# A new emission order and 106 new engine choices for a fused attention and hard-swish MLP kernel

## The chip, the cores and the metric

The kernel runs on one core of a Trainium2 chip. The metric is the device time of one execution in microseconds (us). Three runs of the kernel before gave 426.27, 427.37 and 429.7 us; the median is 427.37 us.

## The reference

Attention over 8 sequences, 12 heads, 448 positions and 64 values per head, with RMS normalisation of queries and keys, and then a two-layer MLP with a hard-swish between the layers:

```
q_n = q / sqrt(mean(q*q) + 1e-6) * g_q          (k likewise)
a   = softmax(q_n @ k_n.T / 8) @ v
x   = a as [8*448, 12*64] = [3584, 768]
h   = x @ w_in                                   [3584, 2048]
out = (h * clip(h + 3, 0, 6) / 6) @ w_out        [3584, 768]
```

Inputs and output are float32 in DRAM; the kernel multiplies in bf16 and sums in float32.

## The kernel before, in words

**Units of work.** Two heads of a sequence make a pair; a sequence has 6 pairs, so pairs P0 to P47 cover the 8 sequences. For a pair, `load` (L417, on the SP queue) fetches k, q and v. `square` (L359 on ACT, L361 on POOL) and a reduction on DVE (L446, L480) give sums of squares, `roots` (L422, L425, on ACT) turns them into factors, and `scale` (L364, on POOL or DVE) writes the normalised bf16 values `qks`. They are turned by TensorE and an identity (L534) for P0 to P12, from P13 on by a transposing DMA on the SP queue (L553, tile T); k is then multiplied by the gains (`kt`, L561 on ACT, L563 on DVE). `score` (L586; L609 in the first sequence) multiplies k by q: two matmuls, one for each head, each on 64 of TensorE's 128 rows. ACT takes the exponential (L592, L614). `av` (L672, L631) multiplies by v with a column of ones, DVE divides (L688, L691), and the result goes into `xT` through TensorE (L656, L707) for the first two sequences and through a transposing DMA (L698) after that.

**The MLP.** `h_group` (L764; L745 in the first sequence) multiplies `w_in` by `xT` in steps of three 448-column matmuls. ACT and DVE apply the hard-swish (L723, L726) into `gT`. `y_group` (L786) multiplies by `w_out` in steps of four 384-column matmuls, ACT or DVE copies the sums out (L345, L347), and the SP queue stores them (L807). The weights come in four parts each, through DMAs that POOL issues (L817, L822); a part of `w_in` serves four of the 16 column blocks of h.

**The first sequence** (P0 to P5) is handled apart: its queries are cut into two halves (z = 0, 1) so that scores can start when half of q is there. 30 groups of four matmuls on zeros (`warm`, L377) stand at the start; some more on zeros (`idle`, L370) stand ahead of `av_first`.

**What sets the order.** Nothing is scheduled at run time. The kernel first makes a list of 2386 plan entries (`Plan.add`), each with its dependencies and the engines that it may run on. `Plan.emit` (L193) then walks a list written out by hand, `ORDER` (L35), and issues each entry on the engine that `WAY` (L23) picks: the first of its list when it has no number there, otherwise the one at that number. The engines take their instructions strictly in that order; semaphores make them wait for one another. The SP queue carries the loads, the transposing DMAs and the stores, also in order.

```python
    def emit(self, order):
        ...
        for i in order:
            kind, engines, fn, preds = self.ops[i]
            fn(engines[WAY.get(i, 0)])
```

The entries that matter below: 0 to 3 are the four parts of `w_in` and 4 to 7 those of `w_out`; 212, 230 and 250 square the second half of q for P0, P2 and P5, 122 the first half for P4; 126 scales the k of P4 and 154 the first half of q for P5; 509 is the exponential of the first score step of P7; 904 is the DMA that turns the result of P17, the last pair of the third sequence, into `xT`.

Of the kernel before, what the change touches and what calls it, by code (L numbers as in the profile page):

```python
# [23 lines left out]
    53: 1, 63: 2, 68: 1, 69: 1, 78: 2, 83: 1, 84: 1, 95: 1, 100: 1, 101: 2, 121: 1, 127: 1, 148: 1, 212: 1,  # L24
    214: 1, 230: 1, 232: 1, 241: 1, 250: 1, 326: 1, 346: 1, 366: 2, 386: 1, 387: 1, 496: 2, 525: 1, 544: 1,
    560: 2, 583: 1, 589: 2, 617: 1, 624: 1, 637: 1, 664: 1, 770: 1, 879: 1, 880: 1, 886: 1, 921: 1, 954: 1,
    1005: 1, 1010: 1, 1017: 1, 1024: 1, 1067: 1, 1108: 2, 1125: 1, 1151: 1, 1160: 1, 1166: 2, 1274: 1, 1286:
    1, 1317: 1, 1324: 1, 1335: 1, 1344: 1, 1350: 1, 1370: 1, 1376: 1, 1393: 1, 1402: 1, 1445: 1, 1469: 1,
    1474: 1, 1530: 1, 1553: 1, 1572: 2, 1598: 1, 1615: 1, 1630: 1, 1641: 1, 1650: 1, 1673: 1, 1708: 1, 1714:
    1, 1754: 1, 1785: 1, 1817: 1, 1822: 1, 1865: 1, 1872: 2, 1891: 1, 1898: 2, 1909: 1, 1918: 1, 1924: 1,  # L30
    1949: 1, 1956: 1, 1972: 1, 1973: 1, 1979: 1, 1987: 1, 2016: 1, 2039: 1, 2067: 1, 2072: 1, 2095: 1, 2114:
    2, 2136: 1, 2151: 1, 2159: 1, 2174: 1, 2195: 1, 2313: 1, 2333: 1, 2374: 1,
# [3 lines left out]
    9, 20, 8, 21, 22, 11, 23, 10, 24, 25, 13, 28, 26, 14, 27, 53, 17, 31, 55, 32, 16, 33, 54, 212, 12, 34,  # L36
    56, 57, 58, 35, 68, 92, 61, 213, 36, 59, 18, 70, 60, 29, 69, 62, 214, 91, 73, 71, 84, 37, 119, 64, 72,
    30, 38, 76, 83, 65, 66, 39, 145, 40, 67, 74, 215, 104, 75, 118, 102, 85, 77, 79, 103, 41, 120, 94, 81,
    80, 15, 86, 82, 95, 63, 129, 87, 225, 105, 42, 89, 96, 43, 44, 19, 88, 130, 131, 93, 108, 110, 111, 109,
    97, 112, 146, 98, 106, 132, 100, 113, 45, 99, 107, 135, 121, 114, 156, 115, 158, 148, 136, 122, 116,  # L40
    133, 157, 46, 117, 90, 134, 47, 123, 149, 159, 172, 164, 0, 48, 150, 124, 230, 174, 125, 165, 232, 49,
    78, 126, 151, 166, 216, 50, 173, 167, 233, 51, 52, 127, 152, 160, 217, 175, 154, 162, 161, 137, 138,
    163, 139, 153, 231, 188, 190, 168, 189, 169, 178, 218, 179, 176, 170, 140, 191, 177, 128, 220, 141, 200,
    221, 219, 142, 234, 201, 202, 171, 143, 340, 227, 192, 193, 144, 203, 194, 101, 195, 224, 303, 155, 196,
    222, 261, 304, 180, 223, 248, 305, 197, 226, 181, 182, 235, 250, 249, 183, 236, 228, 306, 315, 184, 271,
    185, 237, 238, 147, 272, 316, 239, 186, 198, 339, 240, 187, 247, 199, 317, 251, 204, 318, 245, 205, 360,
    341, 327, 244, 307, 308, 252, 206, 241, 309, 253, 207, 328, 242, 273, 254, 208, 329, 209, 246, 255, 256,
    330, 310, 210, 243, 347, 359, 211, 311, 274, 342, 257, 348, 260, 349, 312, 319, 320, 258, 229, 321, 343,
    313, 350, 322, 344, 314, 370, 323, 331, 324, 371, 372, 361, 1, 325, 326, 374, 373, 332, 275, 345, 259,
    351, 375, 333, 352, 334, 362, 353, 363, 354, 335, 386, 397, 364, 336, 376, 398, 355, 337, 263, 377, 276,  # L50
    365, 338, 399, 387, 356, 401, 357, 400, 264, 402, 378, 2, 379, 358, 500, 388, 346, 380, 403, 405, 489,
    501, 406, 381, 407, 265, 404, 408, 266, 389, 382, 277, 409, 490, 502, 383, 506, 390, 410, 503, 384, 267,
    411, 268, 391, 412, 507, 385, 278, 504, 508, 3, 505, 366, 512, 283, 513, 509, 392, 491, 510, 535, 284,
    511, 524, 514, 269, 515, 516, 517, 285, 554, 270, 537, 525, 518, 286, 519, 492, 279, 553, 493, 520, 538,
    521, 280, 393, 555, 522, 281, 291, 495, 536, 292, 523, 282, 494, 539, 498, 293, 543, 526, 287, 367, 544,
    540, 541, 368, 288, 542, 395, 294, 527, 566, 289, 564, 497, 545, 556, 528, 290, 546, 567, 530, 547, 394,
    299, 565, 262, 548, 529, 300, 549, 533, 550, 295, 301, 582, 532, 551, 583, 302, 570, 296, 531, 552, 572,
    571, 421, 297, 4, 573, 568, 593, 298, 569, 595, 6, 584, 413, 414, 594, 415, 618, 422, 423, 416, 596,
    574, 417, 646, 418, 575, 557, 419, 576, 577, 585, 617, 559, 601, 578, 599, 420, 602, 424, 425, 579, 426,
    558, 429, 427, 430, 600, 428, 5, 580, 607, 431, 433, 581, 647, 432, 605, 597, 560, 437, 598, 608, 438,  # L60
    496, 434, 439, 606, 586, 630, 435, 440, 603, 587, 628, 604, 436, 445, 619, 7, 441, 631, 446, 588, 629,
    648, 609, 442, 447, 636, 634, 443, 448, 610, 611, 620, 649, 444, 612, 650, 621, 453, 637, 613, 622, 635,
    614, 659, 657, 652, 449, 658, 450, 623, 454, 451, 660, 615, 455, 738, 663, 616, 452, 632, 748, 737, 750,
    633, 458, 561, 739, 638, 562, 456, 591, 639, 457, 640, 396, 641, 740, 749, 465, 625, 642, 643, 466, 664,
    369, 769, 644, 751, 499, 467, 645, 651, 534, 661, 754, 756, 662, 468, 654, 770, 459, 626, 469, 771, 665,
    590, 666, 757, 667, 760, 668, 477, 821, 669, 772, 670, 773, 741, 460, 755, 589, 743, 671, 478, 672, 461,
    796, 746, 563, 752, 462, 742, 479, 753, 655, 470, 795, 761, 780, 758, 782, 759, 774, 797, 480, 471, 783,
    822, 777, 762, 624, 763, 786, 764, 775, 481, 765, 472, 781, 766, 767, 473, 653, 823, 768, 853, 808, 474,
    784, 806, 482, 776, 824, 785, 812, 483, 854, 787, 825, 809, 484, 745, 485, 880, 627, 798, 788, 486, 789,
    790, 799, 807, 677, 801, 678, 744, 791, 804, 679, 832, 792, 834, 826, 488, 833, 680, 673, 747, 793, 674,  # L70
    835, 800, 813, 685, 675, 827, 803, 810, 879, 840, 676, 838, 844, 686, 811, 855, 681, 687, 682, 839, 779,
    688, 814, 815, 829, 683, 816, 817, 856, 656, 693, 857, 841, 818, 858, 684, 794, 694, 819, 689, 828, 695,
    836, 820, 696, 864, 837, 690, 881, 866, 691, 842, 778, 701, 843, 692, 1050, 870, 702, 845, 867, 697,
    1049, 703, 698, 830, 882, 1017, 846, 704, 859, 592, 847, 848, 865, 1051, 709, 896, 699, 892, 890, 883,
    893, 849, 700, 885, 710, 850, 861, 1052, 851, 705, 711, 1018, 862, 706, 871, 891, 831, 712, 868, 884,
    1030, 1053, 707, 1028, 888, 1019, 717, 869, 860, 887, 718, 708, 852, 1101, 872, 719, 873, 874, 1031,
    875, 720, 713, 802, 1040, 876, 1029, 714, 877, 1102, 725, 897, 715, 1020, 1034, 716, 894, 1021, 1036,
    1022, 895, 1103, 721, 722, 1035, 1076, 1025, 898, 878, 899, 723, 900, 1055, 1037, 901, 724, 726, 902,
    1104, 1054, 903, 1060, 727, 729, 1061, 728, 904, 730, 1023, 1041, 1032, 731, 1062, 1075, 733, 464, 1063,
    732, 734, 1066, 1033, 1077, 905, 735, 1088, 1038, 1058, 1086, 736, 1039, 906, 476, 909, 1078, 1057,  # L80
    1079, 1105, 910, 907, 1081, 1026, 1042, 908, 911, 1043, 1044, 1080, 1087, 913, 912, 1045, 1089, 1133,
    914, 1124, 1046, 1047, 917, 1067, 1106, 918, 915, 463, 1024, 916, 1159, 1064, 1084, 1112, 1114, 1065,
    919, 1092, 1134, 1160, 922, 1068, 1135, 1048, 920, 1113, 1069, 1070, 921, 886, 1118, 1083, 1161, 1136,
    1071, 1286, 923, 889, 924, 863, 1093, 1162, 1318, 1119, 925, 1072, 1073, 1125, 929, 1107, 926, 930,
    1115, 927, 1082, 933, 805, 1285, 931, 934, 1317, 932, 1120, 1144, 1137, 935, 1090, 1138, 937, 1150,
    1091, 936, 938, 1163, 941, 1164, 939, 475, 1094, 940, 1095, 1085, 1121, 1139, 1096, 1097, 1287, 945,
    1110, 1056, 1109, 946, 1098, 1288, 1165, 1145, 1099, 1167, 942, 1319, 1074, 1151, 1146, 1116, 1170, 943,
    947, 1117, 944, 487, 948, 1108, 1320, 1142, 1289, 1321, 1122, 1290, 949, 950, 1100, 1123, 957, 1343,
    1344, 1126, 1308, 1127, 1128, 1345, 1171, 1129, 951, 1147, 952, 1176, 1130, 1131, 953, 1296, 1168, 954,
    1172, 1148, 1141, 958, 1149, 961, 955, 959, 962, 928, 1323, 1370, 960, 1152, 1132, 963, 1153, 1309,  # L90
    1154, 1291, 1297, 1155, 965, 1156, 964, 1173, 966, 1401, 1177, 969, 967, 1157, 970, 968, 1298, 1174,
# [862 lines left out]
```

## Time and profile before

| | us |
|---|---|
| median of three runs | 427.37 |
| the profiled execution | 427.26 |
| its span, first to last instruction | 425.2 |
| PE (matmul) busy | 415.3 |
| ACT busy | 292.1 |
| DVE busy | 220.6 |
| POOL busy | 179.9 |

PE is TensorE's matmuls and PEld its weight loads; DVE is VectorE, ACT ScalarE, POOL GpSimd, SP SyncE. A matmul's recorded duration includes its way through the array, so that neighbours overlap in the records: what a step of PE costs is read from start to start, not from its duration. The granted TensorE clock was full over the whole span. The other 2.1 us of the execution lie around the span.

### The profile page before, as it was taken

The numbers are of one execution on the slowest core, as the hardware profiler recorded it, in microseconds if no ns is written. First come the engines' busy times: TensorE is split into PE (matmuls) and PEld (weight loads), VectorE is DVE, ScalarE is ACT, GpSimd is POOL, SyncE is SP. The second block draws the span as 40 slices with busy tenths as digits, with TensorE's granted clock in tenths as the row PEclk, the third lists the DMA queues.
The fourth block names the chain that finished last, engine by engine and source line by source line (L and its number), as shares of the span: only waits on it lengthen the run. The fifth ranks groups of instructions, "written<-read, shape, count | busy, mean of one in ns | idle before, by whom it ended". The sixth has DMA issues, their size and how long they took to land.

```text
span 425.2 us, 10132 instructions
## 1 busy us (share of the span) xinstructions
PE 415.3 (98%) x4050; PEld 248.5 (58%) x4050; DVE 220.6 (52%) x438; ACT 292.1 (69%) x533; POOL 179.9 (42%) x205
## 2 busy tenths in 40 slices
PE   7899999999999999999999999999999999999996
PEld 6665887554555555555555565555555555655564
DVE  5878777447965664545454555464434432233300
ACT  6899887789998886796867766587865842143211
POOL 4899777685876544446061472223410300000000
PEclk9999999999999999999999999999999999999999
DMA  7999999979969978665765348928530412101214
GB/s 252 295 270 257 225 237 179 298 196 238 246 158 215 243 197 206 158 178 146 164 184 168 69 108 184 239 64 212 124 75 11 113 49 67 49 2 47 66 40 145
DMA packets 98930, 67.76 MB, mean 159 GB/s; under 512 B 53156, under 2 KB 95428, under 8 KB 98884
## 3 DMA queue, kind: packets, MB, share of 16 engines
q1 hardware_dynamic: 93248, 60.50, 55.2%
q0 software_dynamic: 5248, 6.29, 8.9%
q8 instruction: 31, 0.51, 0.5%
q10 hardware_dynamic: 388, 0.34, 0.3%
q14 instruction: 15, 0.12, 0.1%
HBM read 50.23 MB, written 11.01 MB: 144 GB/s over the span
## 4 chain that ended last, share of the span: by engine, by line
PE 79%; DMA 8%; ACT 4%; DVE 3%; POOL 2%; issue 2%; SPq 1%; DVEq 0%; ACTq 0%; POOLq 0%
PE M L786 26%; PE M L764 24%; PE X L672 8%; PE S L586 5%; PE S L786 5%; PE M L745 4%; PE X L586 2%; DMA w_in_sb<-in_moe_w_in_dram 2%; ACT eT L614 2%; DMA gT<-in_q_dram 2%; DMA T<-qks 2%; PE X L764 1%; DMA qk<-in_k_dram 1%; POOL sq L361 1%; PE S L764 1%
## 5 line engine op out<-in xcount | busy, mean ns | idle before, releaser
L786 PE MATMUL M<-w_out_sb,gT 128*128 128x384 bf16 x752 | 137.8, 326 | 0.0
L364 POOL TENSOR_TENSOR qks<-qk,rs 112x512 bf16<-112x512 f32 (+1 forms) x90 | 91.5, 1030 | 104.2 <-ACT rs L425 57.9
L764 PE MATMUL M<-xT,w_in_sb 128*128 128x448 bf16 x618 | 134.4, 353 | 0.4 <-ACT y L345 0.2
L726 DVE SCALAR_TENSOR_TENSOR gT<-ts,M 128x448 bf16<-128x448 f32 x119 | 73.1, 617 | 90.4 <-ACT ts L723 89.4
L786 PEld LDWEIGHTS <-gT 128*128 128x128 bf16 x912 | 84.2, 98 | 57.7 <-issue 7.2
L592 ACT ACTIVATE eT<-S 112x896 bf16<-112x896 f32 x112 | 100.0, 916 | 7.7 <-PE S L586 5.0
L764 PEld LDWEIGHTS <-w_in_sb 128*128 128x128 bf16 x672 | 60.3, 98 | 57.8 <-issue 11.7
L723 ACT ACTIVATE ts<-M 128x448 f32<-128x448 f32 x119 | 64.6, 544 | 40.1 <-PE M L764 29.6
L361 POOL TENSOR_TENSOR sq<-qk 112x512 f32<-112x512 f32 (+1 forms) x60 | 60.7, 1019 | 40.0 <-DVE ssq L446 12.4
L592 ACT ACTIVATE eT<-X 112x896 bf16<-112x896 f32 x56 | 51.4, 918 | 17.6 <-PE X L586 16.8
L672 PEld LDWEIGHTS <-eT 112*128 112x128 bf16 x1344 | 53.2, 97 | 15.7 <-issue 2.2
L672 PE MATMUL X<-va,eT 112*128 112x65 bf16 x1344 | 56.8, 194 | 0.0
L446 DVE TENSOR_REDUCE ssq<-sq 112x16 f32<-112x1024 f32 x42 | 50.8, 1213 | 10.5 <-POOL sq L361 7.3
L586 PE MATMUL S<-T 64*128 64x448 bf16 x224 | 35.6, 353 | 0.0
L345 ACT COPY y<-M 128x384 f32<-128x384 f32 x28 | 13.4, 479 | 28.9 <-PE M L786 24.5
L691 DVE TENSOR_TENSOR xn<-X,rd 112x512 bf16<-112x512 f32 x42 | 28.9, 689 | 1.1
L586 PEld LDWEIGHTS <-T 64*128 64x128 bf16 x336 | 12.6, 94 | 24.4 <-issue 18.5
L745 PE MATMUL M<-xT,w_in_sb 128*128 128x224 bf16 x192 | 23.1, 259 | 0.6 <-DMA w_in_sb<-in_moe_w_in_dram 0.3
L347 DVE COPY y<-M 128x384 f32<-128x384 f32 x19 | 10.5, 554 | 25.2 <-PE M L786 21.5
L359 ACT ACTIVATE sq<-qk 112x512 f32<-112x512 f32 (+1 forms) x37 | 21.5, 590 | 2.6 <-DMA qk<-in_k_dram 2.2
L688 DVE RECIPROCAL rd<-X 112x8 f32<-112x8 f32 x42 | 8.6, 205 | 28.0 <-PE X L672 25.1
L786 PE MATMUL S<-w_out_sb,gT 128*128 128x384 bf16 (+1 forms) x128 | 22.9, 316 | 0.0
(84 smaller groups left out, 303.5 us busy)
## 6 DMA issues: line engine op xcount, KB each, us to landing
qk<-in_k_dram SPq DMA_DIRECT2D x45, 256.0 KB, 3.8
qk<-in_q_dram SPq DMA_DIRECT2D x45, 256.0 KB, 4.2
vf<-in_v_dram SPq DMA_DIRECT2D x45, 256.0 KB, 4.0
w_in_sb<-in_moe_w_in_dram POOLq DMA_DIRECT2D x4, 768.0 KB, 8.8
w_out_sb<-in_moe_w_out_dram POOLq DMA_DIRECT2D x4, 768.0 KB, 8.8
out_dram<-y SPq DMA_DIRECT2D x7, 336.0 KB, 3.9
out_dram<-y SPq DMA_DIRECT2D x8, 288.0 KB, 3.2
out_dram<-y SPq DMA_DIRECT2D x8, 240.0 KB, 3.6
```

The lines of the kernel that those rows point to most:

```text
L361: em(nc.gpsimd.tensor_tensor(out=out, in0=in_, in1=in_, op=A_MULT))
L364: em((nc.vector if e == DVE else nc.gpsimd).tensor_tensor(out=out, in0=in_, in1=by.unsqueeze(3).to_broadcast(list(in_.shape)), op=A_MULT))
L446: em(nc.vector.tensor_reduce(out=ssq[:].rearrange("p i n -> p (i n)"), in_=sq[:].rearrange("p i (n d) -> p (i n) d", d=D), axis=AX_X, op=A ...
L586: em(nc.tensor.matmul(out=ps[:, a, 0:S], lhsT=qkT[r, S + t * TP:S + t * TP + 128], rhs=qkT[r, 0:S], start=True, stop=True))
L592: em(nc.scalar.activation(out=eT[:, t, 0:S2].rearrange("p (a s) -> p a s", a=2), in_=ps[0:TP, :, 0:S], func=EXP, bias=0.0, scale=1.0))
L672: em(nc.tensor.matmul(out=X_ps[:, a, i * E1:(i + 1) * E1], lhsT=eT[:, t, c:c + 128], rhs=va[:, a, t, :], start=(t == 0 and i == 0), stop=( ...
L691: em(nc.vector.tensor_tensor(out=xn[:].rearrange("p i a d -> p a i d"), in0=view()[:, :, :, 0:D], in1=rd[:].unsqueeze(3).to_broadcast([TP, ...
L723: em(nc.scalar.activation(out=ts[:], in_=ps()[:, 0:S], func=RELU, bias=0.5, scale=1.0 / 6.0))
L726: em(nc.vector.scalar_tensor_tensor(out=out, in0=shape(ts[:]), scalar=1.0, in1=shape(ps()[:, 0:S]), op0=A_MIN, op1=A_MULT))
L745: em(nc.tensor.matmul(out=ps()[:, f * SH:(f + 1) * SH], lhsT=w_in_sb[:, kt, f0:f0 + 128], rhs=xT[:, kt, z * SH:(z + 1) * SH], start=(kt == ...
L764: em(nc.tensor.matmul(out=ps()[:, 0:S], lhsT=w_in_sb[:, kt, f * 128:(f + 1) * 128], rhs=xT[:, kt, :], start=(kt == 0), stop=(kt == NKT - 1)))
L786: em(nc.tensor.matmul(out=ps()[:, 0:nc0], lhsT=gT[:, f, i * 128:(i + 1) * 128], rhs=w_out_sb[:, f, c0:c0 + nc0], start=(f == 0), stop=(f = ...
```

## The change

Only the two lists change. The computation, the tiles, the plan entries and their dependencies are the same. 1947 of the 2386 places of `ORDER` hold another entry; the last 337 places are the same, and on PE nothing differs after the records at 307.9 us of the profile. `WAY` gives 106 entries another engine.

```diff
 WAY = {
-    53: 1, 63: 2, 68: 1, 69: 1, 78: 2, 83: 1, 84: 1, 95: 1, 100: 1, 101: 2, 121: 1, 127: 1, 148: 1, 212: 1,
...
+    53: 1, 63: 2, 68: 1, 69: 1, 83: 1, 84: 1, 95: 1, 100: 1, 101: 1, 121: 1, 122: 1, 126: 1, 127: 1, 128: 2,
+    148: 1, 154: 1, 155: 2, 212: 1, 214: 1, 232: 1, 346: 2, 386: 1, 387: 1, 393: 2, 457: 1, 474: 1, 481: 1,
...
 ORDER = [
-    9, 20, 8, 21, 22, 11, 23, 10, 24, 25, 13, 28, 26, 14, 27, 53, 17, 31, 55, 32, 16, 33, 54, 212, 12, 34,
...
-    133, 157, 46, 117, 90, 134, 47, 123, 149, 159, 172, 164, 0, 48, 150, 124, 230, 174, 125, 165, 232, 49,
...
-    313, 350, 322, 344, 314, 370, 323, 331, 324, 371, 372, 361, 1, 325, 326, 374, 373, 332, 275, 345, 259,
...
+    9, 20, 8, 21, 22, 11, 23, 10, 24, 25, 14, 28, 26, 13, 27, 53, 17, 31, 55, 32, 16, 33, 54, 56, 92, 34,
...
+    0, 150, 52, 124, 165, 125, 137, 173, 174, 127, 138, 126, 166, 151, 234, 162, 152, 139, 175, 154, 160,
...
+    370, 274, 331, 1, 321, 371, 332, 258, 322, 333, 259, 372, 323, 362, 345, 324, 374, 363, 373, 275, 375,
...
```

Read through the plan, the entries that change engine are these (each number counts entries):

| kind of entry | moves |
|---|---|
| square, 512 or 256 wide | 20 POOL to ACT, 17 ACT to POOL |
| cast of v to bf16 | 10 POOL to DVE, 5 DVE to POOL, 5 ACT to POOL, 4 ACT to DVE, 3 DVE to ACT, 3 POOL to ACT |
| copy of y out of PSUM | 11 ACT to DVE, 4 DVE to ACT |
| kt | 7 ACT to DVE, 5 DVE to ACT |
| copies of T and xT out of PSUM | 7 DVE to ACT, 3 ACT to DVE |
| scale (126 and 154) | 2 POOL to DVE |

And the stretches of the lists that the prediction speaks of:

| list | before | after |
|---|---|---|
| POOL, between the first and the second part of `w_in` | 17 entries | 14: the two scales 126 and 154 and two casts (P4, P5) are gone, 250 has come |
| ACT, up to entry 509 | 75 entries | 72: 230, 250, two half copies out of PSUM and a cast are gone, 122 and another cast have come |
| ACT, entry 212 | second on ACT, ahead of the first roots | 15th on ACT, right ahead of the first exponential |
| PE, stretches of consecutive score entries | 92 | 88 |
| SP, work on PE between 904 and its first reader | 4.2 us | 3.4 us |
| all engines, entries | PE 989, ACT 535, DVE 396, POOL 194, SP 272 | PE 989, ACT 530, DVE 409, POOL 186, SP 272 |

The 30 groups of `warm` are the same; 24 of them stand ahead of P1's first score (19 before), 25 ahead of P2's (23), 29 ahead of P3's (25), all ahead of P4's (as before).

229 rows, old and new, of tables (ORDER, WAY) are left out of this document.

## The prediction

> **What bounds the kernel now.** I read the page's head and slices first, then busy time by stage, then the timeline of each engine where PE stands still.
>
> ```profile
> span 425.2 us, 10132 instructions
> PE 415.3 (98%) x4050; PEld 248.5 (58%) x4050; DVE 220.6 (52%) x438; ACT 292.1 (69%) x533; POOL 179.9 (42%) x205
> ```
>
> PE is busy 98% of the span, so the rest looks like 10 us. A finer count says more. In PE's timeline I took the start-to-start time of every plan entry and, for each kind, the one that it has when nothing delays it: 0.650 us for a y step, 0.568 for a hidden step, 0.244 for an av step, 0.198 for a score step of two matmuls. With two surcharges for scores (below) these sum to 408.05 us; from the first matmul's start to the last one's it took 420.3. The difference, 12.3 us, is waiting: 9.4 us of it before 42 us, 2.9 us in the 380 us after. So the order can win in two places only: the first tenth of the span, and PE's own steps.
>
> Busy time by stage (length, then PE, PEld, DVE, ACT, POOL, the clock, DMA share, GB/s) shows who is full early:
>
> ```profile
> 0.00:10.60 10.60, 7.84 (x98) 6.85 (x98) 5.31 (x21) 6.72 (x19) 5.06 (x17) 1.00 0.78 252
> 10.60:21.30 10.70, 8.84 (x154) 6.52 (x153) 9.06 (x25) 9.40 (x23) 9.09 (x12) 1.00 1.06 295
> 21.30:42.50 21.20, 19.98 (x331) 13.35 (x332) 17.63 (x53) 20.94 (x39) 20.05 (x25) 1.00 1.08 264
> 85.00:104.00 19.00, 18.94 (x195) 10.37 (x190) 11.83 (x21) 16.58 (x31) 13.03 (x15) 1.00 0.89 210
> 104.00:123.50 19.50, 19.45 (x191) 10.17 (x190) 16.08 (x30) 18.59 (x34) 15.25 (x16) 1.00 0.92 207
> ```
>
> From 21.3 to 42.5 us ACT is busy 20.94 of 21.20 us, POOL 20.05, and the DMA engines are full. That stretch is set by ACT's list and by POOL's, which issues the weights. On PE its end looks like this:
>
> ```profile
> 40.31 0.35 PE L586 MATMUL S<-T 64*128 64x448 bf16 x2
> 40.64 0.36 PE L534 MATMUL S<-identity,qks 112*128 112x112 bf16 x4
> 41.32 0.75 PE L745 MATMUL M<-xT,w_in_sb 128*128 128x224 bf16 x6 [0.32 <-DMA w_in_sb<-in_moe_w_in_dram]
> ```
>
> The step at 41.32 waits for the second part of `w_in`, which POOL issued at 32.35 (next fence) and which took 8.92 us in the chain.
>
> ```profile
> 31.36 1.04 POOL L364 TENSOR_TENSOR qks<-gT,rs 112x512 bf16<-112x512 f32 x1 [0.54 <-POOL sq L361]
> 32.35 0.88 POOL L817 DMA_DIRECT2D w_in_sb<-in_moe_w_in_dram  x1
> ```
>
> The surcharge that a score costs is seen later, where nothing waits:
>
> ```profile
> 153.69 0.73 PE L764 MATMUL M<-xT,w_in_sb 128*128 128x448 bf16 x3
> 154.35 0.36 PE L586 MATMUL S<-T 64*128 64x448 bf16 x2
> 154.55 0.35 PE L586 MATMUL X<-T 64*128 64x448 bf16 x2
> 154.74 0.35 PE L586 MATMUL S<-T 64*128 64x448 bf16 x2
> 155.02 1.48 PE L786 MATMUL M<-w_out_sb,gT 128*128 128x384 bf16 x8
> ```
>
> The hidden step ahead of the scores takes 0.66 us start to start (0.568 elsewhere), two scores 0.20 and 0.19, the last one 0.28. So each unbroken stretch of scores costs 0.095 us on the way in and 0.086 on the way out, 0.18 in all, however long it is.
>
> **The change part by part.**
>
> *Score stretches.* PE's list has 92 of them before and 88 after: 4 x 0.18 = 0.72 us less. They lie after 42 us (at the second part of `w_in` both lists hold 30.9 us of PE work), where PE waits 2.9 us in 380, so the saving reaches the end. **-0.72.**
>
> *ACT's list to the first exponential of P7* (at 41.33 us). Out go two half squares (0.41 each), two half copies (0.34, 0.37) and a cast (0.62); in come a half square and a cast: 1.03 - 2.15 = -1.12. Neighbours on ACT overlap by about 0.1 (an exponential lasts 0.91 and the next starts after 0.80), and there are three fewer: -0.82 net. Entry 212, which ran at 4.31 us in a hole of ACT, moves ahead of the first exponential, where ACT has no hole: +0.41. The square of P5's k, for which ACT waits,
>
> ```profile
> 13.72 0.62 ACT L359 ACTIVATE sq<-qk 112x512 f32<-112x512 f32 x1
> 15.04 0.63 ACT L359 ACTIVATE sq<-gT 112x512 f32<-112x512 f32 x1 [0.71 <-DMA gT<-in_k_dram]
> ```
>
> goes behind one more exponential, but its load also moves two places back on SP: between 0 and -0.71, I take -0.5, as an exponential is 0.91 long and two loads on SP issue in about 1. Together **-0.9** (-0.4 to -1.1).
>
> *POOL's list to the second part of `w_in`.* Between the first and second part two scales (1.03, 0.61) and two casts (0.61 each) go, a half square (0.61) comes: -2.26; ahead of the first part it holds 0.61 more. So the second part could be issued 1.65 us earlier. Against it: the two scales now run on DVE beside POOL's. Where that happened before,
>
> ```profile
> 13.05 0.42 DVE L364 TENSOR_TENSOR qks<-qk,rs 112x256 bf16<-112x256 f32 x1
> 13.15 1.22 POOL L364 TENSOR_TENSOR qks<-qk,rs 112x512 bf16<-112x512 f32 x1 [0.17 <-POOL qks L364]
> ```
>
> POOL's took 1.22 us instead of its mean of 1.03: +0.18 each, so about 1.3 us earlier, landing near 40.0. That is more than ACT's 0.9: ACT decides and POOL adds nothing. The Trainium skill speaks harder against this move (SBUF — State Buffer, section Who interferes with whom): a DVE instruction with two SBUF inputs and a GpSimd one that reads SBUF share a port pair, and the later one is blocked for the whole of the earlier. By it POOL would lose the scales' full time, about 0.72 + 0.46 us, the weights would come only 0.5 us earlier, and the sum would be 426.1; the row above shows a partial loss, 0.18 of an overlap of 0.32.
>
> *DVE* gets 1.8 us more by 34 us (the two scales, half copies). It stands idle 5.2 us between 10.6 and 42.5, which covers it; without that cover it would eat up to the whole 0.9.
>
> *After 42 us*: from 84 to 104 us DVE gets 4.6 us more (2 y copies of 0.55, 3 casts of 0.76, a kt, a copy), POOL 2.9 (two squares, two scales, two casts less), ACT 0.2. That makes DVE 16.4, ACT 16.8, POOL 15.9 of 19: a stage as full as the next one was before (16.1, 18.6, 15.3 of 19.5), in which PE waited 0.3 us in all. So between 0 and +0.3; I take 0, as POOL then gets 2.7 less from 104 to 123. Of the rest of the 106 moves ACT gives up about 1.5 us and POOL 7, DVE takes 9.5, all beside a full PE: 0 while DVE is at 52%.
>
> *SP's queue.* I compared, for each transfer, PE's own work between its issue and its first reader. Lower quartiles: loads 5.0 us before, 4.9 after; transposes into T 4.0 and 4.8; stores against the reuse of y 8.5 and 10.3; the least lead of the last weights 9.2 and 12.4. These cost 0. One gets tighter: the DMA that turns P17 into `xT`, 4.2 to 3.4 us ahead of the first hidden step of the third sequence. Such a transfer lands in 2.3 to 7.0 us (median 3.0). Its issue ran within 116.7 to 120.2 us, its reader at 122.74; if it started at about 118.9 it had some 0.9 us to spare and keeps 0.1. I take 0; the bound is +4.0.
>
> *The zero matmuls* fill PE's holes before 20 us; moved forward they delay a score by at most one group (0.22 us) and ACT is behind anyway: 0.
>
> Sum: 427.26 - 0.72 - 0.9 = **425.6 us**. The profiled execution stands 0.11 below the median of the runs.
>
> **The rivals.**
> - *Nothing gained early.* DMA is at 1.06 to 1.08 of its engines from 10.6 to 42.5 us; if the weights land no earlier because of that, PE still waits until 41.3, and only the score stretches count: 427.26 - 0.72 = 426.5. For it: the full DMA. Against: two loads fewer stand ahead of them.
> - *P17's transpose comes late* (slower). PE is in order, and the third sequence's first hidden step holds up everything behind it. With a landing of 7.0 us instead of 3.0 PE stands for 4.0: 425.6 + 4.0 = 429.6. It decides from 3.0 + 0.1 + 1.6 (the gain) = 4.7 us on. For it: 7.0 occurs in the trace. Against: in its stage (85 to 135 us) the median is 2.9 and the most 4.9.
> - *More of ACT's early idle time goes.* From its first square at 3.61 to 42.5 us ACT idles 3.1 us (6.99 - 5.44 up to 10.6 without the 1.28 of a table load, then 1.30 and 0.26). If half of it goes beside the -0.82: 427.26 - 0.72 - 0.82 - 1.55 = 424.2. For it: a list made anew for just this stretch. Against: the waits are for first loads, which cannot come sooner.
>
> **How the numbers follow.** Forecast 50% (own range 425.0 to 426.3), nothing gained early 20%, late transpose 18%, more idle time gone 12%. The range goes from a little under the last rival to the slow one: 423.7 to 429.6. A measurement of this kernel tells about 1% from no change, here 423.1 and 431.6. Under 423.1 takes nearly all of ACT's idle time: 6%. Over 431.6 takes the slow rival and a second late transfer: 8%. Within 1%: 86%.
>
> **What would show it.** Right: 88 entries into scores, the second part of `w_in` issued near 31 us, the step after it on PE near 40.4 instead of 41.3, waits on PE after 42 us still near 2.9 us, a span near 423.5. Wrong: PE idle at the first hidden step of the third sequence with the `xT` transfer as releaser, POOL scales of 1.5 us or more beside DVE's, a first exponential much later than 10 us, or new waits between 84 and 123 us.

## The result, and the profile after

The kernel after the change takes 425.38 us, the median of 15 runs (423.12 to 426.9), beside 428.12 us of the kernel before in the same runs. The ratio on record, which is not quite the quotient of the two medians (0.9936), is 0.9931, with a 95% interval of 0.9916 to 0.9947. The prediction was 425.6 us and "within 1%". The profiled execution took 426.24 us, the second longest of the 15, so it shows the change at a bad moment: 1.02 us below the profiled one of before, where the medians differ by 2.7.

The page's head, and busy time by stage (columns as before; 70 to 85 us is new):

```profile
span 424.5 us, 10158 instructions
PE 415.4 (98%) x4050; PEld 250.2 (59%) x4050; DVE 227.9 (54%) x459; ACT 288.7 (68%) x528; POOL 173.6 (41%) x197
```

```profile
0.00:10.60 10.60, 8.54 (x95) 7.91 (x96) 4.58 (x19) 5.92 (x17) 4.92 (x17) 1.00 0.81 255
10.60:21.30 10.70, 9.43 (x162) 7.09 (x160) 9.82 (x29) 9.89 (x27) 8.53 (x11) 1.00 1.01 299
21.30:42.50 21.20, 20.84 (x348) 14.52 (x347) 18.64 (x57) 20.61 (x35) 20.29 (x25) 1.00 1.09 243
70.00:85.00 15.00, 15.00 (x156) 8.82 (x154) 9.47 (x17) 10.60 (x22) 6.73 (x8) 1.00 1.10 277
85.00:104.00 19.00, 17.26 (x180) 9.37 (x179) 13.23 (x29) 14.93 (x27) 14.17 (x15) 1.00 0.87 200
104.00:123.50 19.50, 19.50 (x192) 10.04 (x191) 15.25 (x31) 18.29 (x34) 13.04 (x15) 1.00 0.91 222
```

PE does more before 42.5 us (38.8 us busy, 36.7 before), and it lost 1.7 us from 85 to 104, where it had been full. The step of `w_in` that PE waited for at 41.32 now starts at 40.06, and the load that it needs is issued at 31.55 instead of 32.35. PE's timeline and POOL's:

```profile
39.23 0.37 PE L588 MATMUL S<-T 64*128 64x448 bf16 x2
39.70 0.36 PE L536 MATMUL S<-identity,qks 112*128 112x112 bf16 x4
40.06 0.75 PE L747 MATMUL M<-xT,w_in_sb 128*128 128x224 bf16 x6
```

```profile
18.07 1.01 POOL L819 DMA_DIRECT2D w_in_sb<-in_moe_w_in_dram  x1
19.85 1.22 POOL L366 TENSOR_TENSOR qks<-gT,rs 112x512 bf16<-112x512 f32 x1 [0.77 <-issue]
...
30.57 1.04 POOL L366 TENSOR_TENSOR qks<-gT,rs 112x512 bf16<-112x512 f32 x1
31.55 0.88 POOL L819 DMA_DIRECT2D w_in_sb<-in_moe_w_in_dram  x1
```

The idle time of 0.32 us at the `w_in` step is gone; the part that it needs has landed at 40.01, level with the end of the transposes ahead of it. The new cost is at 90 to 101 us. On PE:

```profile
93.38 1.15 PE L674 MATMUL X<-va,eT 112*128 112x65 bf16 x32 [0.77 <-DVE va L345]
94.98 1.93 PE L766 MATMUL M<-xT,w_in_sb 128*128 128x448 bf16 x9 [0.44 <-DVE y L349]
...
100.91 1.86 PE L766 MATMUL M<-xT,w_in_sb 128*128 128x448 bf16 x9 [0.54 <-DVE gT L728]
```

All three wait for DVE, which itself waited, and so did POOL:

```profile
92.63 0.69 DVE L345 TENSOR_SCALAR_CACHE_REDUCE va<-vf 112x512 bf16<-112x512 f32 x1 [1.62 <-DMA vf<-in_v_dram]
...
93.25 1.22 DVE L448 TENSOR_REDUCE ssq<-sq 112x16 f32<-112x1024 f32 x1
94.38 0.55 DVE L349 COPY y<-M 128x384 f32<-128x384 f32 x1
```

```profile
91.87 1.04 POOL L363 TENSOR_TENSOR sq<-qk 112x512 f32<-112x512 f32 x1 [2.73 <-DMA qk<-in_k_dram]
```

The v of P13 and the k of P19 arrive late, DVE stands, and what is queued behind it on DVE (a reduction, then a y copy) goes to PE late. Two of these instructions were ACT's before, the cast of P13's v (entry 624) and the y copy (entry 481). ACT's timeline before:

```profile
86.86 0.62 ACT L345 CAST va<-vf 112x512 bf16<-112x512 f32 x1
87.37 0.49 ACT L345 COPY y<-M 128x384 f32<-128x384 f32 x1
```

The change put both on DVE, and it issues the load of that v at 86.61 us instead of 74.24.

To compare kernels I use PE's lag: the time at which a certain plan entry starts on PE, less PE's own work ahead of it (the undelayed time of each step, and 0.18 us for each score stretch). Before: 11.26 us at about 70 us, 11.67 at 104, 13.05 at 319. After: 9.43, 12.32, 13.15. So the profiled execution gains 1.8 us by 70 us, gives back 2.5 by 104, gains 0.55 later; the own work is 0.72 us less (407.33 instead of 408.05), and the time around the span 0.3 less.

### The profile page after: what moved, and what is told of

Its sections match the earlier page's. It is cut to its first block, busy times and chain, and to the rows that moved or that the text cites. A ratio compares the mean times of both kernels' runs of the same rounds, so it can differ in the third digit from the quotient of the medians.

```text
span 424.5 us, 10158 instructions
## 1 busy us (share of the span) xinstructions
PE 415.4 (98%) x4050; PEld 250.2 (59%) x4050; DVE 227.9 (54%) x459; ACT 288.7 (68%) x528; POOL 173.6 (41%) x197
## 4 chain that ended last, share of the span: by engine, by line
PE 84%; DMA 7%; ACT 2%; DVE 2%; POOL 2%; SPq 1%; issue 1%; POOLq 0%; DVEq 0%; ACTq 0%
PE M L788 29%; PE M L766 28%; PE X L674 8%; PE S L588 5%; PE S L788 5%; DMA w_out_sb<-in_moe_w_out_dram 3%; PE X L588 3%; DMA qk<-in_k_dram 3%; DMA gT<-in_k_dram 2%; PE X L766 1%; PE S L766 1%; PE X L788 1%; PE S L611 1%; PE XF L633 1%; SPq L419 1%; DVE ssq L448 1%
## 5 line engine op out<-in xcount | busy, mean ns | idle before, releaser
L788 PE MATMUL M<-w_out_sb,gT 128*128 128x384 bf16 x752 | 139.5, 326 | 0.3 <-DMA w_out_sb<-in_moe_w_out_dram 0.3
L366 POOL TENSOR_TENSOR qks<-qk,rs 112x512 bf16<-112x512 f32 (+1 forms) x89 | 90.5, 1032 | 84.5 <-ACT rs L427 44.3
L766 PEld LDWEIGHTS <-w_in_sb 128*128 128x128 bf16 x672 | 60.3, 98 | 57.7 <-issue 11.9
L363 POOL TENSOR_TENSOR sq<-qk 112x512 f32<-112x512 f32 (+1 forms) x56 | 56.7, 1018 | 59.7 <-DMA qk<-in_q_dram 29.9
L588 PE MATMUL S<-T 64*128 64x448 bf16 x224 | 34.3, 353 | 0.0
L349 DVE COPY y<-M 128x384 f32<-128x384 f32 x26 | 14.4, 553 | 31.0 <-PE M L788 28.2
L361 ACT ACTIVATE sq<-qk 112x512 f32<-112x512 f32 (+1 forms) x41 | 23.8, 589 | 3.2 <-DMA qk<-in_k_dram 3.0
L347 ACT COPY y<-M 128x384 f32<-128x384 f32 x21 | 10.0, 478 | 22.2 <-PE M L788 18.3
## 6 DMA issues: line engine op xcount, KB each, us to landing
w_out_sb<-in_moe_w_out_dram POOLq DMA_DIRECT2D x4, 768.0 KB, 11.9
```

What stands on the lines that cost most here:

```text
L361: em(nc.scalar.square(out=out, in_=in_))
L363: em(nc.gpsimd.tensor_tensor(out=out, in0=in_, in1=in_, op=A_MULT))
L366: em((nc.vector if e == DVE else nc.gpsimd).tensor_tensor(out=out, in0=in_, in1=by.unsqueeze(3).to_broadcast(list(in_.shape)), op=A_MULT))
L588: em(nc.tensor.matmul(out=ps[:, a, 0:S], lhsT=qkT[r, S + t * TP:S + t * TP + 128], rhs=qkT[r, 0:S], start=True, stop=True))
L766: em(nc.tensor.matmul(out=ps()[:, 0:S], lhsT=w_in_sb[:, kt, f * 128:(f + 1) * 128], rhs=xT[:, kt, :], start=(kt == 0), stop=(kt == NKT - 1)))
L788: em(nc.tensor.matmul(out=ps()[:, 0:nc0], lhsT=gT[:, f, i * 128:(i + 1) * 128], rhs=w_out_sb[:, f, c0:c0 + nc0], start=(f == 0), stop=(f = ...
```

## The experiments

What had to be told apart, in the words used by the expectations:

- **A**: the gain is the early lists (ACT's and POOL's, up to some 43 us) plus 0.18 us for each score stretch; the waits at 85 to 104 us are a loss of the new list that could be mended.
- **B**: the gain is made later, or is the luck of one execution.
- **C**: up to about 110 us something else than PE sets the pace, so an early gain is given back.
- **D**: the waits at 85 to 104 us belong to the profiled execution and cost the medians nothing.
- **E** and **F** are named where they are tried.

All were timed in five rounds against the kernel before; ratios are to it, with 95% intervals.

### The two kernels again

No edit (before2, after2).

> The kernel before, unchanged, for a second trace of it. Theory A (the gain comes early, from ACT's and POOL's lists, and from fewer score stretches; in the profiled execution some 2 us of it were lost again between 85 and 104 us): ratio 1.000; PE waits about 9.4 us before 42 us and about 0.3 us from 85 to 104 us, as in the first trace. Theory B (the early waits of one execution are chance, the profile of one execution says little): the waits before 42 us differ by over 1 us from 9.4.

> The changed kernel, unchanged, for a second trace of it. Theory A: ratio near 0.993; PE waits about 8 us before 42 us and again 1.5 to 2.5 us from 85 to 104 us, because the load of P13's v is issued late in every execution. Theory B: the wait from 85 to 104 us was one execution's bad luck with a DMA and is under 0.5 us here.

Measured: before2 1.0005 (0.9987 to 1.0023); after2 0.9937 (0.9914 to 0.9959), 424.84 us. The gain repeats in new runs, so it is not one execution's luck. After2's profiled execution was the longest of its six (426.95) and had the `w_in` step at 41.04 us, before2's at 42.41: this early point moves by 1 us from one execution to the next in both kernels. That is B's sign for before2, whose waits ahead of 42 us were 1.1 us longer than before's. From 85 to 104 us after2's lag grew by 0.95 us, between what A (1.5 to 2.5) and B (under 0.5) had said, and by 2.4 in after: part of the loss in the first profile was that execution's own.

### Score stretches

15 stretches of three scores are broken in two after the second score, the order otherwise that of after:

```diff
 ORDER, PE's entries, one of 15 places
- 1262, 1608, 1610, 1580, 1265, 1266
+ 1262, 1608, 1610, 1265, 1580, 1266
```

(1608, 1610 and 1580 are scores, 1265 a y step.)

> The changed kernel, with 15 of its unbroken stretches of three scores between 210 and 318 us broken in two: a hidden or y step goes ahead of the third score. 103 stretches instead of 88, the same work. Theory A (each stretch costs PE 0.18 us, and PE sets the end there): 15 x 0.18 = 2.7 us over the changed kernel, ratio to the kernel before 0.998 to 1.001. Rival (a stretch's surcharge is hidden, fewer stretches are no part of the gain): ratio 0.992 to 0.995, as the changed kernel.

Measured: 1.0048 (1.0026 to 1.0069), 429.63 us, more than expected. PE's own work, which counts 0.18 us for each stretch, rose from 407.33 to 410.03. The trace bears the price out directly: at 12 of the 15 places the second score takes 0.285 us instead of 0.189 start to start, and the step put ahead of the third about 0.756 instead of 0.660 (a y step) or 0.674 instead of 0.578 (a hidden step). The rest is waiting from 170 to 319 us: the lag grows by 2.6 us there (10.98 to 13.58) and by 0.4 in after; two waits of av steps for ACT's exponentials, 0.34 us each, are part of it, and most of it is not explained. So stretches cost at least their 0.18 us.

### Halves of the list

Four hybrids of the two lists, each with the engine choices that belong to its entries:

```diff
 ORDER
- the new list
+ h_new_old: 597 places new (on PE to 74 us of its trace), then old;  h_old_new: 604 places old, then new
+ h43_new_old: 394 places new (to about 43 us), then old;  h43_old_new: to 43 us old, then new
```

> The first 597 places of the new order with their new engines (up to the first score of P12, about 71 us), then all the rest in the order and on the engines of before. Theory A: the early gain stays (P12's first score 1.2 us earlier than in the kernel before), 92 score stretches, no loss from 85 to 104 us: 1.2 to 1.9 us under the kernel before, ratio 0.9955 to 0.997. Theory B (the gain is made later, by order and engines of the rest): ratio 0.999 to 1.001.

> The first 604 places of the order of before with its engines (up to the first scores of P12), then all the rest in the new order and on the new engines. Theory A: no early gain, 88 score stretches (-0.7 us), the loss from 85 to 104 us there: 0 to 1.5 us over the kernel before, ratio 1.000 to 1.0035. Theory B: most of the gain, ratio 0.994 to 0.996.

> The first 394 places of the new order with their engines (up to about 43 us, ahead of the parts of w_out), then the order and engines of before; 93 score stretches. Theory A (what is won early on ACT's and POOL's lists reaches the end): 0.7 to 1.7 us under the kernel before, ratio 0.996 to 0.9985. Theory C (engines other than PE set the pace up to some 110 us, so an early lead is given back in new waits there): ratio 0.999 to 1.001, and the trace shows more waiting of PE between 43 and 125 us than the 1.5 to 2.3 us of the kernel before.

> The old list and choices up to the PE step at about 43 us, the new ones from there on; 87 stretches of scores. If the parts add: the early gain of 1.2 to 1.7 us is missing, the stretches (0.7 to 0.9 us) and what the new list saves after 104 us stay: 0.996 to 0.998. If all of the gain were made before 43 us: 0.999 to 1.001. If none of it were made there (rival B): 0.992 to 0.9945.

Measured: h_new_old 0.9997 (0.9974 to 1.0019), h43_new_old 0.9994 (0.9968 to 1.0020), h_old_new 0.9971 (0.9953 to 0.9989), h43_old_new 0.9982 (0.9960 to 1.0005). Without the early new list 0.2 to 0.3% remains, 0.8 to 1.2 us: the stretches' 0.72 and little else. The missing 0.35 to 0.5% (1.5 to 2.1 us) goes with the early part. (A had expected h_old_new to be slower than the kernel before, by the loss at 85 to 104 us; that loss is not there, its lag grows by 0.1 us from 70 to 104.) The other two hybrids do not show that gain alone: both miss A's range and lie in that of B or C. C's sign is not there either: in h43_new_old PE's lag grows by 1.2 us from 43 to 125 us, in before by 1.5. The early gain was not made in their profiles, whose `w_in` steps start at 42.33 and 41.73 us: POOL's square of P7 waited for its load, ahead of the second part of `w_in`, though the load was issued as in after (24.12 and 24.60 us, 24.79 in after). Here h_new_old, the slowest execution of its twelve (430.66 us), which waits for `w_out` besides:

```profile
30.88 1.04 POOL L356 TENSOR_TENSOR sq<-qk 112x512 f32<-112x512 f32 x1 [2.24 <-DMA qk<-in_q_dram]
31.88 1.04 POOL L359 TENSOR_TENSOR qks<-gT,rs 112x512 bf16<-112x512 f32 x1
32.86 0.88 POOL L812 DMA_DIRECT2D w_in_sb<-in_moe_w_in_dram  x1
```

In after that wait was 0.22 us, in after2 0.33, in split 0.91, in fix_v (below) 0, in h43_new_old 1.68. Whether it is long in the hybrids by chance, and whether the old later list would keep an early gain, stays open.

### The late loads

fix_v swaps loads on the SP queue, so that P13's v goes earlier; `loads` does that too and moves P7's q ahead; fix_wout issues the first three parts of `w_out` earlier.

```diff
 ORDER, fix_v: entries trade places
- ... 563 ... 592 ... 396, 534
+ ... 396 ... 534 ... 563, 592
 ORDER, loads: fix_v, and
- 227, 226, 224
+ 224, 227, 226
 ORDER, POOL's entries, fix_wout
- 554, 582, 583, 4, 5, 6
+ 4, 554, 5, 582, 6, 583
```

> The changed kernel with four loads of v exchanged on SP's queue: P13's with P16's and P15's with P17's, so that P13's and P15's are issued about 8 and 3 us earlier. Theory A (PE's wait at P13's av and the waits right behind it come from that late load): 0.8 to 2 us under the changed kernel, ratio to the kernel before 0.9885 to 0.9915. Theory D (only an execution that is being profiled has that wait): no change to the changed kernel, ratio 0.9925 to 0.994, though the profile's wait from 85 to 104 us falls under 0.7 us.

> After with five loads of the SP queue in another order: v of P13 trades places with v of P16, v of P15 with v of P17, and q of P7 goes ahead of q of P8 and v of P7. Theory A (the lone late load of P13 costs what the profiled execution shows, about 0.9 us, and POOL's square of P7 waits 0 to 1 us for its q by chance): 0.5 to 1.3 us below after, ratio to before 0.990 to 0.992. Rival D (that wait exists in the profiled execution only, and other engines set the end there): as after, 0.9925 to 0.994.

> The changed kernel with the first three parts of w_out issued one, two and three squares earlier on POOL, 2 to 4 us sooner than in the changed kernel. Theory A: PE's wait of 0.5 us at the third y step (part 2 of w_out) goes: 0.3 to 0.6 us under the changed kernel, ratio 0.9915 to 0.9925. Theory C (other waits take its place): ratio 0.993 and the wait reappears within the next 35 us.

Measured: fix_v 0.9923 (0.9897 to 0.9949), loads 0.9937 (0.9913 to 0.9961), fix_wout 0.9980 (0.9955 to 1.0004). All three miss A's ranges, fix_v narrowly. Neither of the first two can be told from after (0.9931), although P13's v came in time: there D is right on the time, or close to it, but its reason is not borne out. In `loads` the same stage still loses 2.3 us of lag, in a profiled execution of 424.48 us that is one of the fastest of its twelve; the waits have moved to the next late transfer. (fix_v loses 0.7 us from 85 to 104 us, but 1.4 from 70 to 85, where PE waits 1.21 us for a part of `w_out`.) In `loads`, on PE, POOL and SP:

```profile
92.92 2.08 PE L760 MATMUL M<-xT,w_in_sb 128*128 128x448 bf16 x9 [0.85 <-DVE y L343]
...
99.14 1.86 PE L760 MATMUL M<-xT,w_in_sb 128*128 128x448 bf16 x9 [0.68 <-DVE gT L722]
```

```profile
90.11 1.04 POOL L357 TENSOR_TENSOR sq<-qk 112x512 f32<-112x512 f32 x1 [2.53 <-DMA qk<-in_k_dram]
```

```profile
84.22 0.47 SPq L413 DMA_DIRECT2D qk<-in_k_dram  x1
```

And h43_old_new, whose PE is 2.5 us later at about 70 us (68.57 against 66.10 for the same entry), POOL and SP:

```profile
90.44 1.04 POOL L357 TENSOR_TENSOR sq<-qk 112x512 f32<-112x512 f32 x1 [0.46 <-DMA qk<-in_k_dram]
```

```profile
86.29 0.45 SPq L413 DMA_DIRECT2D qk<-in_k_dram  x1
```

In `loads` DVE reduces that square at 91.18 us and copies y, queued behind it, at 92.32, for which PE's step at 92.92 waits. The k of P19 is issued 2.1 us earlier in `loads` and lands at nearly the same moment: 5.9 us from issue to use instead of 4.1. Six profiles with the new later list (loads, split, scales_back, fix_v, h43_old_new, after2) issue it between 84.22 and 86.54 us and use it between 90.11 and 90.44; the DMA engines are full from 70 to 85 us (1.02 to 1.12 in them). Three do not fit: ways_back (below) uses it at 89.54, after at 91.87, fix_wout at 94.08. That speaks for C, with the transfers as what paces: from 70 to 104 us h_old_new gives back 0.1 us, h43_old_new 0.4, ways_back 1.1, scales_back and after2 1.5, fix_v 2.1, loads 2.3, the more the earlier PE is; after (2.9) and split (1.1) stand apart. It is read from profiles. No run took transfers away, and none put the y copy and the cast (entries 481 and 624) back on ACT; so it is not told apart whether the late loads cost this by themselves, or only because the change queued PE's y copy behind them on DVE.

fix_wout made it worse. A square behind the moved parts went late, and PE stood for 1.11 us until 58.16. Then POOL waited 3.36 us for P13's k, whose load was issued at 51.35 us, as in after (51.53, no wait there), and PE stood for 1.21 us until 65.22. Its profiled execution was the longest of its twelve (429.41 us, median 426.88).

### The early engine choices

scales_back puts entries 126 and 154 on POOL again; ways_back undoes all ten choices that stand ahead of the second part of `w_in`. The order is that of after.

```diff
 WAY, scales_back
- 126: 1, 154: 1
 WAY, ways_back
- 78: 0, 101: 1, 122: 1, 126: 1, 128: 2, 154: 1, 155: 2, 230: 0, 241: 0, 250: 0
+ 78: 2, 101: 2, 122: 0, 126: 0, 128: 0, 154: 0, 155: 0, 230: 1, 241: 1, 250: 1
```

> After with the two scales 126 and 154 back on POOL: the order is untouched, POOL has two instructions more ahead of the second part of w_in and DVE two less. Theory A (what is gained by 70 us hangs on that part, which the step at 40 us needs): POOL's list is about 1.3 us longer, the part is issued near 32.8 instead of 31.5, the step starts near 41.3 instead of 40.1, and the time goes up by about 1.2 us: ratio to before 0.995 to 0.9975. Rival E (ACT's list decides, as the prediction has it, and the step only fills a place that would otherwise be filled by a wait behind it): the step is late, the time is not: 0.992 to 0.9945.

> After with all ten early engine choices (entries 78, 101, 122, 126, 128, 154, 155, 230, 241 and 250, all ahead of the second part of w_in) as they were before; the order of the new list stays. Theory A: the gain up to 70 us comes from the engines' lists, so most of its 1.2 to 1.7 us goes and the score stretches' 0.7 us stays: 0.9955 to 0.9985. Rival F (it comes from the order of the entries, not from their engines): 0.992 to 0.9945.

Measured: scales_back 0.9951 (0.9931 to 0.9972), ways_back 0.9985 (0.9960 to 1.0009), 425.5 and 426.62 us, beside `loads` at 424.72 on the same chip. So A holds against F in the times: with the old choices most of the early gain is gone, although the new order stays. (The profiled execution of ways_back is a fast one, 425.39 us, and has its `w_in` step at 40.48, so that its trace shows less of the loss.) Of the two scales, the medians cannot decide between A and E, and POOL's timeline shows that the edit did not do what both take for granted, to make the part late. scales_back:

```profile
17.67 1.01 POOL L813 DMA_DIRECT2D w_in_sb<-in_moe_w_in_dram  x1
18.70 1.06 POOL L360 TENSOR_TENSOR qks<-qk,rs 112x512 bf16<-112x512 f32 x1
19.71 1.61 POOL L360 TENSOR_TENSOR qks<-gT,rs 112x256 bf16<-112x256 f32 x2
...
31.62 0.88 POOL L813 DMA_DIRECT2D w_in_sb<-in_moe_w_in_dram  x1
```

POOL does both scales and still issues the second part 13.95 us after the first, at 31.62, against 13.48 and 31.55 in after, where it has nothing to do at that place but wait: its next scale, P5's, needs the roots that ACT finishes at 19.71 (19.50 + 0.21), and POOL starts it at 19.85. Without the wait for P7's load (0.28 us in scales_back, 0.22 in after) the two lengths are 13.67 and 13.26, and 13.21 to 13.29 in six more profiles with the scales on DVE (after2 has 14.30, by 1.05 us more of waiting for P5's roots). So the 1.64 us taken off POOL's list gave about 0.4 us.

What releases PE's `w_in` step can be read from all 14 profiles. In 11 it starts 0.045 to 0.047 us after the second part has landed; in h_new_old, ways_back and loads 0.25 to 1.45 us after. PE in after2:

```profile
40.40 0.36 PE L536 MATMUL S<-identity,qks 112*128 112x112 bf16 x4
41.04 0.75 PE L747 MATMUL M<-xT,w_in_sb 128*128 128x224 bf16 x6 [0.29 <-DMA w_in_sb<-in_moe_w_in_dram]
```

So at this step it is mostly the part that comes last, by POOL's issue and a landing of 8.0 to 9.1 us. The way to the step had to shorten too: the transposes ahead of it on PE end at 41.00 us in before and at 40.06 in after.

The starts move by 1 us and more from one execution to the next. These are lengths, from each profile:

| kernel | ratio | first to second part of `w_in` | first exponential to entry 509 |
|---|---|---|---|
| before | 1 | 15.22 | 31.70 |
| before2 | 1.0005 | 16.27 | 33.05 |
| h_new_old | 0.9997 | 15.53 | 32.53 |
| h43_new_old | 0.9994 | 14.93 | 31.65 |
| h43_old_new | 0.9982 | 15.22 | 31.68 |
| h_old_new | 0.9971 | 15.21 | 32.09 |
| ways_back | 0.9985 | 14.88 | 31.54 |
| scales_back | 0.9951 | 13.95 | 30.82 |
| after | 0.9931 | 13.48 | 30.29 |
| after2 | 0.9937 | 14.63 | 30.59 |
| fix_v | 0.9923 | 13.21 | 29.96 |
| loads | 0.9937 | 13.21 | 30.09 |
| fix_wout | 0.9980 | 13.72 | 30.31 |
| split | 1.0048 | 14.16 | 30.91 |

Between kernels the time follows the two columns roughly, fix_wout and split apart, which lose their time later. The columns go together, so they don't tell ACT's list from POOL's. A length varies as well: the same kernel twice differs by 1.05 and 1.15 us in the first column and by 1.3 and 0.3 in the second. POOL waited 1.05 us ahead of its first scale in before2 instead of 0.02, and 1.82 in after2 instead of 0.77.

## Why the prediction was right, and where not

- **Score stretches, -0.72**: right. 88 stretches, and broken stretches cost 0.18 us each; PE's own work, 408.05 and 407.33, is reckoned with that price.
- **ACT's list, -0.9**: right in the profiled execution. The first exponential came at 10.05 us instead of 9.63 (+0.42, +0.41 predicted), entry 509 at 40.34 instead of 41.33: -0.99. In the second pair of profiles it came at 41.03 instead of 42.69, -1.66, so that an agreement to 0.1 us is luck; the direction is not.
- **POOL's list, 1.3 us earlier**: 0.80 (31.55 instead of 32.35). The work was counted well: between the two parts POOL's instructions take 2.0 us less (13.9 to 11.8; 1.9 predicted). But its waits there grew from 1.36 to 1.65 us instead of staying: 0.54 ahead of its last scale went (the prediction's fence), 0.77 ahead of P5's scale came. So the scales gave about 0.4 us instead of 1.28, since the roots of P5 come no earlier. And the first part was issued 0.94 later (18.07 against 17.13; 0.61 predicted).
- **"ACT decides"**: not what the traces show. The step started at 40.06 (40.4 predicted), when the second part of `w_in` had just landed, and in most profiles that part comes last. It was 1.26 us earlier, so the early gain was 1.3 us at that point and 1.8 by 70 us, against 0.9. The sum had nothing for 42 to 70 us, where PE's lag grew by 0.9 us before and by 0.3 after. The other profiles agree: 0.8 to 0.9 with the old list there, 0.3 to 0.4 with the new one, fix_wout apart.
- **84 to 104 us, "0 to +0.3"**: wrong. The lag grows by 2.9 us from 70 to 104 us in after and by 0.4 in before; in after2, and in three relatives whose profiles lie within 0.4 us of their medians (scales_back, fix_v, loads), by 1.5 to 2.3. New waits here were one of the prediction's own signs of being wrong. Its sign of being right, waits after 42 us still near 2.9 us, failed too: they were 1.3 us longer than in before. I took busy sums of DVE, ACT and POOL as the limit, and they were even lower than I had expected (13.2, 14.9, 14.2 of 19). What failed is the step from busy time to no wait. I compared quartiles of the transfers' leads, and a few loads came late; DVE, to which the change had moved a y copy and the cast behind these loads, then stood idle while PE waited for what is behind.
- **P17's transpose, 0**: right. The stretch with the third sequence's first hidden step shows no idle time:

```profile
122.13 0.35 PE L588 MATMUL X<-T 64*128 64x448 bf16 x2
122.42 1.88 PE L766 MATMUL M<-xT,w_in_sb 128*128 128x448 bf16 x9
```

- **Scales side by side**: POOL's took 1.22 us at 19.85 beside DVE's (1.04 to 1.06 alone), the 0.18 that the sum had, once and not twice. In ways_back, where POOL's started first, it was DVE's that took longer (DVE, then POOL):

```profile
18.50 1.07 DVE L360 TENSOR_TENSOR qks<-qk,rs 112x256 bf16<-112x256 f32 x1
```

```profile
18.24 1.03 POOL L360 TENSOR_TENSOR qks<-qk,rs 112x512 bf16<-112x512 f32 x1 [0.49 <-ACT rs L421]
```

  DVE's 0.43 (in scales_back, while POOL issues) became 1.07: it lost 0.64 of the 0.77 us in which POOL's was running. The Trainium skill's rule (SBUF — State Buffer, Who interferes with whom), that the later one is blocked, fits this row nearly in full, and POOL's only by half (0.17 of 0.32 us).

So the number came out right by two errors that partly cancel, and with luck. Early, PE gained more than the 0.9 us: against before and before2 (lags of 11.26 and 12.27 at about 70 us), scales_back, fix_v and loads stand at 9.68, 8.96 and 8.26. Then the stage up to 104 us took back 1.5 to 2.3 us. At 319 us these three have lags of 12.01, 11.92 and 11.39, against 13.05 and 14.30: about 1.9 us less (means of 11.77 and 13.68), and with the stretches' 0.72 that makes 2.6, near the 2.7 between the medians. Forecast were 1.6 us. This account is argued from relatives: the kernel's own two profiles, both of slow executions, have 13.15 and 13.66 at 319 us, which with the 0.72 makes 1.0. And the 425.6 us came so close to 425.38 only because the kernel before took 428.12 us in these runs, not the 427.26 that the sum starts from; 1.6 us under 428.12 would be 426.5.

## What to carry to other kernels

Taking work off an engine gains only what that engine does not then wait: look at what its next instruction needs (here P5's roots) before counting the full duration. A gain made early must be followed to the next stretch in which another resource is full (here the transfers at 70 to 85 us), where part of it can be given back; check there each transfer's lead by itself, and what stands behind its first reader in that engine's list. Compare medians of many runs, and more than one profile of each kernel: here both a start and the length between two points differed by 1 us between two executions of the same kernel, over a third of the whole gain.

## What the runs showed of the hardware

- A transfer issued earlier beside full DMA engines landed hardly earlier: the k of P19 took 5.9 us from issue to its use when issued at 84.22 (loads) and 4.1 when issued at 86.29 (h43_old_new). Four more profiles fit this, three do not.
- The median landing of a `w_out` part is 11.9 us in after and 8.8 in before. The new list has POOL issue three of them in a row from 54.56 us, the old one two from 54.00, then one at 59.55. h_new_old, three in a row too, had 13.5, and there, in the slowest execution of its twelve, PE waited 1.57 and 1.24 us for two of them:

```profile
73.26 0.81 PE L781 MATMUL M<-w_out_sb,gT 128*128 128x384 bf16 x4 [1.57 <-DMA w_out_sb<-in_moe_w_out_dram]
77.02 0.81 PE L781 MATMUL M<-w_out_sb,gT 128*128 128x384 bf16 x4 [1.24 <-DMA w_out_sb<-in_moe_w_out_dram]
```
